# Weight slabs of a decode kernel's last pass, fetched in four half-megabyte pieces through a two-half ring

## The chip, the cores and the metric

The kernel runs on one core of one Trainium2 chip, as one launch. The metric is device time in microseconds (us), as a median of several runs; before the change it is 1956.27 us, the median of three runs (1954.14 to 1961.74). A profile of one further execution shows where that time goes. MB is a million bytes in the rates that the profile states; a "megabyte" of a tile or a slab is 1024 KB.

## The reference

Four layers are applied to one token's vector of 1024 values: attention over a cache, a feed-forward layer, the same attention again, the same feed-forward layer again. All gradients are wanted too, those of the two large caches included.

```python
# attention: 32 query heads, 4 cache groups, 65536 cached rows of 128
q = layernorm(x) @ wq                         # wq: 1024 x 4096
p = softmax(q @ k_cache.T * Dh ** -0.5)
x = x + (p @ v_cache) @ wo                # wo: 4096 x 1024
# feed-forward: w1 1024 x 3584, w2 3584 x 1024
x = x + relu(layernorm(x) @ w1 + b1) ** 2 @ w2 + b2
...
out, vjp = jax.vjp(f, x, k_cache, v_cache, wq, wo, w1, b1, w2, b2)
grads = vjp(grad_out)
```

Each cache is 4 x 65536 x 128 in bf16. Their gradients have the same shape and are summed over both attention layers.

## The kernel before, in words

The work is done in four passes over the two caches with dense stages between them: a forward pass for each attention layer, a backward pass for the second one, and a last pass (`attn_bwd4`, L1268) that does the backward work of the first attention layer and writes the cache gradients of both.

**The last pass.** It walks over 256 items, 64 for each of the four groups, of eight cache columns each. Four items are a block, and one block of either cache is one DMA of 1024 KB into one slot. For each item the V columns are turned on TensorE (`vT`, L1324) and multiplied with the output gradient (`vS`, L1355); the result on VectorE is X (L1373); X and the stored probabilities are turned (L1339), and outer products form the gradients of V and K (`outer16`, L1396), which ScalarE or VectorE (`evac`, L161 and L164) copies from PSUM to slots that GpSimd's queue stores (L1402). At the end `k8` (L1427) multiplies the K columns with X. `pipeline` (L828) emits these stages item by item; a scheduler then sets the order on every engine. So an "item" in what follows is counted by the groups of eight matmuls of L1427 that stand in the built program's order.

**Slots.** All of these tiles lie in one arena of 20 slots of 1024 KB (L255 to L261). `take_one` (L284) gives a load the slot that has been free longest, of those that are not set aside for stores (up to five are). Loads are all issued by SyncE's queue (SP), in order: a load whose slot is still in use holds up those behind it.

**Background work.** `Background.step` (L774) runs once an item. It advances an "urgent" generator by one step; if that step answers "wait", the turn goes on to the "normal" work: outer products of the weight gradients (`g_outer`, L1499, and `g_outer_wide`, L1518, in steps of one `rank2`, L1468). Any other answer uses up the turn. What is left of either is run to its end by `drain` (L808), called from `fill4` (L1837) ten items before the end of the pipeline.

**The urgent work of the last pass** is six products of a vector with a weight block of 2 MB: three of wo (`g_dO`, L953, for the groups still to come) and three of wq (`g_dn`, L980, for the groups that are done). Both go through `g_rowdots` (L565). The weight block comes as two slabs of 1024 KB, each with four rows of 1024 values in every partition, through `slabs` (L433), whose DMA is L450. A row is multiplied with the broadcast vector on VectorE (L586, into `mv_t`, of which there are two buffers), and ScalarE sums the product (L575). In this pass four "wait" steps lie ahead of the first slab's products, after the broadcast's four, and eight between the request of the second slab and its products:

```python
        for kc, slab in slab_it:
            if vbc is None:
                vbc = yield from g_bcast_vec(vcol, nj)
                for _ in range(steps - WAIT_STEPS + 1):
                    yield "wait"
            elif kc % 4 == 0:
                for _ in range(steps):
                    yield "wait"
```

A slab's slot is freed when the generator comes back after its fourth row, and the second slab is then requested into another slot. The functions that the diff touches, and their callers:

Of the kernel before, what the change touches and what calls it, by code (L numbers as in the profile page):

```python
# [10 lines left out]
BF = mybir.dt.bfloat16  # L11
F32 = mybir.dt.float32
ACTF = mybir.ActivationFunctionType
ALU = mybir.AluOpType
AX = mybir.AxisListType
PSUM = bass.MemoryType.PSUM
P = 128
# [3 lines left out]
def kernel(  # L21
# [24 lines left out]
    nc = tc.nc  # L46
# [6 lines left out]
    R = HQ // G  # L53
    F = B_w1.shape[1]
    DC, FC = D // P, F // P
# [10 lines left out]
    TLEAD = 2  # L66
    STORE_STEPS = 5
    WAIT_STEPS = 5
    NSLOT = 12
    NWT = 6  # L70
    NKEEP = [8, 7, 7]
# [3 lines left out]
    vec = ctx.enter_context(tc.tile_pool(name="vec", bufs=1))  # L75
    tmp = ctx.enter_context(tc.tile_pool(name="tmp", bufs=2))
    ktpool = ctx.enter_context(tc.tile_pool(name="ktpool", bufs=4))
    mvs = ctx.enter_context(tc.tile_pool(name="mvs", bufs=2))
# [3 lines left out]
    PS = {}  # L82
# [62 lines left out]
    def add_load(act=0.0, dve=0.0, pe=0.0):  # L145
        load["act"] += act
        load["dve"] += dve
        load["pe"] += pe
# [107 lines left out]
    JW = 2 * J  # L256
    NG = NSLOT + 2 * G
    assert C * R == BLK
# [9 lines left out]
    def plane(lay, g):  # L268

        return NSLOT + G + g if lay else NSLOT + G - 1 - g  # L270

# [155 lines left out]
    def rows_of(W):  # L427
        return W.rearrange("(kc p) n -> p kc n", p=P)
# [4 lines left out]
    def slabs(name, load, nk, kper, ncols, ahead=1, flat=False):  # L433
        pend = deque()
        ks = deque(range(0, nk, kper))

        def fetch():
            k = ks.popleft()
            i = None
            if ks and flat and NOW["wide"] and not odd_one():  # L440
                i = take_pair()
            if i is None:
                kn = min(kper, nk - k)
                sl = Slot(name)
            else:
                kn = min(2 * kper, nk - k)
                ks.popleft()
                sl = Slot(name, at=i, both=True)
            v = sl.t[:, 0:kn * ncols].rearrange("p (k n) -> p k n", n=ncols)
            nc.sync.dma_start(out=v, in_=load(k, kn))  # L450
            pend.append((k, kn, sl, v))

        def gen():
            while ks or pend:
                while ks and len(pend) < ahead:
                    fetch()
                k, kn, sl, v = pend.popleft()
                for kk in range(kn):
                    NOW["slab"] = sl
                    yield k + kk, v[:, kk, :]  # L460
                sl.over = True
                if not sl.users:
                    sl.free()
        g = gen()
        g_fetch = [fetch for _ in range(ahead)]
        return g, g_fetch
# [8 lines left out]
    def wq_slabs(g, ahead=1):  # L475
        v = rows_of(A_wq)
        return slabs("s_wq", lambda k, kn: v[:, k:k + kn, g * 1024:(g + 1) * 1024], DC, 4, 1024, ahead, True)
# [5 lines left out]
    def wo_runs(g):  # L483

        v = A_wo[g * 1024:(g + 1) * 1024, :].rearrange("(p k) n -> p k n", k=8)
        return slabs("s_wo", lambda k, kn: v[:, k:k + kn, :], R, 4, 1024, 1, True)[0]
# [9 lines left out]
    def g_mv(slab_it, nk, nbk, xcol, ps_of, finish, side=None, pre=None, cols=d_cols):  # L496
# [4 lines left out]
        for kc, slab in slab_it:  # L501
            if ps_of is ps_bg and kc % 4 == 0:
                for _ in range(WAIT_STEPS):
                    yield "wait"
# [42 lines left out]
    def g_bcast_vec(vcol, nj):  # L547
        pt = ps_mv([nj, P], F32)
        nc.tensor.transpose(pt[:, :], vcol, ident_f[:, :])
        yield  # L550
        rows = tmp.tile([32, P], BF, name="bc_rows")
        nc.vector.tensor_copy(out=rows[0:nj, :], in_=pt[:, :])
        vbc = mvs.tile([P, nj * P], BF, name="vbc", tag="vbc", bufs=1)
        yield
        for j0 in range(0, nj, 4):
            pg = ps_gg() if PS["pass4"] else ps_tr([P, 512], F32)
            for jj in range(4):
                nc.tensor.matmul(pg[:, jj * P:(jj + 1) * P], lhsT=ident_b[0:nj, j0 + jj:j0 + jj + 1].to_broadcast([nj, P]),
                                 rhs=rows[0:nj, :], start=True, stop=True)
            nc.scalar.copy(out=vbc[:, j0 * P:(j0 + 4) * P], in_=pg[:, 0:512])  # L560
            add_load(act=0.6)
            yield
        return vbc

    def g_rowdots(slab_it, nk, vcol, nj, finish, name):  # L565
        n = nj * P
        y = vec.tile([P, nk], F32, name=name)
        nc.gpsimd.memset(y[:], 0.0)
        vbc = None
        due = None  # L570
        steps = 8 if PS["pass4"] else WAIT_STEPS

        def total(t, kc):
            def f():
                nc.scalar.activation(out=t[:, :], in_=t[:, :], func=ACTF.Copy, accum_out=y[:, kc:kc + 1])  # L575
            return f
        for kc, slab in slab_it:
            if vbc is None:
                vbc = yield from g_bcast_vec(vcol, nj)
                for _ in range(steps - WAIT_STEPS + 1):  # L580
                    yield "wait"
            elif kc % 4 == 0:
                for _ in range(steps):
                    yield "wait"
            t = mvs.tile([P, n], BF, name="mv_t", tag="mv_t", bufs=2)
            nc.vector.tensor_tensor(out=t[:, :], in0=slab, in1=vbc[:, :], op=ALU.mult)  # L586
            add_load(dve=0.1 + n * 0.00054, act=0.42 + n * 0.00083)
            if due is not None:
                due()
            due = total(t, kc)  # L590
            yield
        due()
        yield
        r = finish(y[:, :])
        if r is not None:
            yield from r
        yield
# [299 lines left out]
    def gsl(g):  # L897
        return slice(g * R, (g + 1) * R)
# [35 lines left out]
    def dO_finish(L, g):  # L934
        def fin(y):
            nc.vector.tensor_copy(out=L["dOT"][:, gsl(g)], in_=y)
            prod = tmp.tile([P, R], F32, name="dlt_prod")
            nc.vector.tensor_tensor(out=prod[:], in0=L["dOT"][:, gsl(g)], in1=L["oT"][:, gsl(g)], op=ALU.mult)
            yield
            pd = ps_mv([33, R], F32)  # L940
            nc.tensor.matmul(pd[:, :], lhsT=ones_f[:, 0:33], rhs=prod[:, :], start=True, stop=True)
            yield
            negd = tmp.tile([33, R], F32, name="negd")
            nc.vector.tensor_scalar(out=negd[:], in0=pd[:], scalar1=-1.0, scalar2=None, op0=ALU.mult)
            hi = tmp.tile([33, R], BF, name="negd_hi")
            nc.vector.tensor_copy(out=hi[:], in_=negd[:])
            lo = tmp.tile([33, R], BF, name="negd_lo")
            nc.vector.tensor_tensor(out=lo[:], in0=negd[:], in1=hi[:], op=ALU.subtract)
            nc.vector.tensor_copy(out=L["nd2"][0:1, gsl(g)], in_=hi[0:1, :])
            nc.vector.tensor_copy(out=L["nd2"][32:33, gsl(g)], in_=lo[32:33, :])  # L950
        return fin

    def g_dO(L, dx, g):  # L953
        def fin(y):
            each = tmp.tile([P, R, 8], F32, name="run_own", bufs=1)
            nc.vector.tensor_tensor(out=each[:, :, :], in0=y.unsqueeze(1).to_broadcast([P, R, 8]),
                                    in1=M8[:, :].unsqueeze(2).to_broadcast([P, R, 8]), op=ALU.mult)
            yield
            pt = ps_mv([P, R, 8], F32)
            nc.tensor.matmul(pt[:, :, :].rearrange("p r k -> p (r k)"), lhsT=from_runs[:, :, :].rearrange("p a b -> p (a b)"),  # L960
                             rhs=each[:, :, :].rearrange("p r k -> p (r k)"), start=True, stop=True)
            yield
            own = tmp.tile([P, R, 8], F32, name="run_own", bufs=1)
            nc.vector.tensor_tensor(out=own[:, :, :], in0=pt[:, :, :], in1=eighth[:, :].unsqueeze(1).to_broadcast([P, R, 8]), op=ALU.mult)
            back = tmp.tile([P, R], F32, name="run_o")
            nc.vector.tensor_reduce(out=back[:], in_=own[:, :, :], axis=AX.X, op=ALU.add)
            yield
            yield from dO_finish(L, g)(back[:, :])
        yield from g_rowdots(wo_runs(g), R, dx[:], DC, fin, "%s_dO%d" % (L["name"], g))


    def dn_finish(dn, first):
        def fin(y):
            if first:
                nc.vector.tensor_copy(out=dn[:], in_=y)
            else:
                nc.vector.tensor_tensor(out=dn[:], in0=dn[:], in1=y, op=ALU.add)
        return fin

    def g_dn(L, dn, g, first):  # L980
        yield from g_rowdots(wq_slabs(g)[0], DC, L["dqT"][:, gsl(g)], R, dn_finish(dn, first), "%s_dn%d" % (L["name"], g))


# [894 lines left out]
```

## Time and profile before

| what | value |
|---|---|
| median of three runs | 1956.27 us (1954.14 to 1961.74) |
| the profiled execution: time / span from first to last instruction | 1956.67 us / 1954.7 us |
| TensorE's granted clock, mean of the span | 0.911 |
| busy share: PE / VectorE (DVE) / ScalarE (ACT) / GpSimd | 82% / 60% / 53% / 7% |
| moved by DMA over the whole span | 787.64 MB, mean 403 GB/s |
| last pass, 1195 us to the end at 1955 us | 760 us for 256 items |
| products L586 in the last pass | 48, median 682 ns |
| sums L575 in the last pass | 48, median 1070 ns, and as many reads of the sum, 203 ns |
| SP's waits in the last pass for PE's L1427 / L1324 / for DVE's L586 | 384.4 us (47 times) / 129.3 us (40) / 23.0 us (6) |

The page gives busy time by engine, then the span in 40 slices, then the DMA queues, a chain of what ended last, the costliest groups and the DMA issues. A line of a group names the source line, the engine, the tiles (out<-in), how often, and the mean duration; after the bar stands how long the engine sat idle ahead of these instructions and what ended that. The same can be asked for any stretch of the span, and each engine's instructions can be listed in order of time, with the idle time ahead of each in brackets. A wait there is put down to what came last by the profile; "issue" means that nothing the profile shows ended it.

### The profile page before, as it was taken

How to read it: one execution, taken by the hardware profiler on the slowest of the kernel's cores; microseconds unless marked ns; L12 is line 12 of the kernel's file. 1: busy time of each engine (PE TensorE's matmuls, PEld its weight loads, DVE VectorE, ACT ScalarE, POOL GpSimd, SP SyncE). 2: the span in 40 equal slices, each digit the busy share in tenths (PEclk: the TensorE clock that was granted, in tenths of full speed). 3: DMA queues.
4: the chain of work that ended last, by engine and by line, in shares of the span. 5: the costliest groups of instructions: out<-in, count | busy, mean ns of one | idle time of the engine just before them, and what ended most of it. 6: DMA issues, size and time to landing. Idle time of an engine off the chain costs nothing. (4 is left out here: it accounts for less than half of the span.)

```text
span 1954.7 us, 67155 instructions
## 1 busy us (share of the span) xinstructions
PE 1598.7 (82%) x30319; PEld 1312.0 (67%) x30319; DVE 1167.6 (60%) x2421; ACT 1038.3 (53%) x1600; POOL 141.2 (7%) x321
## 2 busy tenths in 40 slices
PE   6878788687888878887787898888996987687977
PEld 6878778687777778777777785555554554454644
DVE  5655455255455544544454476867776886676866
ACT  3444334254334444435363465766876785576765
POOL 0000000000000000000000001111111211121211
PEclk9989899699899999898998999888888998897997
DMA  9999999999999998899999987999999999899997
GB/s 395 426 426 425 428 428 410 401 399 425 429 425 428 428 412 307 317 427 423 426 426 418 403 321 297 411 404 423 423 424 405 420 423 423 341 423 384 424 422 317
DMA packets 105997, 787.64 MB, mean 403 GB/s; under 512 B 9312, under 2 KB 16494, under 8 KB 42094
## 3 DMA queue, kind: packets, MB, share of 16 engines
q1 hardware_dynamic: 81630, 617.65, 76.6%
q0 software_dynamic: 24080, 165.70, 20.4%
q8 instruction: 237, 3.88, 0.7%
q14 instruction: 50, 0.41, 0.1%
HBM read 617.62 MB, written 165.69 MB: 401 GB/s over the span
## 5 line engine op out<-in xcount | busy, mean ns | idle before, releaser
L164 DVE COPY kt<-ps_tr 128x1024 bf16<-128x1024 bf16 x724 | 496.6, 688 | 439.5 <-PE ps_tr L1012 246.6
L161 ACT CAST arena<-ps_gg 128x1024 bf16<-128x1024 f32 x457 | 444.3, 1011 | 190.9 <-PE ps_gg L1396 147.0
L1012 PE MATMUL ps_tr<-ident_b,arena 128*128 128x128 bf16 x3840 | 309.0, 226 | 39.1 <-DMA arena<-in_A_k_cache_dram 26.6
L161 ACT COPY kt<-ps_tr 128x1024 bf16<-128x1024 bf16 x164 | 171.8, 1053 | 187.1 <-PE ps_tr L1204 118.1
L164 DVE CAST arena<-ps_gg 128x1024 bf16<-128x1024 f32 (+2 forms) x186 | 222.3, 1195 | 79.9 <-PE ps_gg L1396 35.0
L1012 PEld LDWEIGHTS <-arena 128*128 128x128 bf16 x3840 | 232.8, 101 | 47.9 <-DMA arena<-in_A_k_cache_dram 29.4
L1114 PE MATMUL ps_acc<-arena 128*128 128x64 bf16 (+4 forms) x4096 | 205.8, 196 | 61.5 <-DMA arena<-in_A_v_cache_dram 49.3
L1396 PE MATMUL ps_gg<-GG,xt 64*128 64x512 bf16 x1024 | 212.2, 412 | 47.5 <-DVE arena L164 35.0
L1114 PEld LDWEIGHTS <-arena 128*128 128x128 bf16 x4096 | 159.8, 101 | 66.3 <-DMA arena<-in_A_v_cache_dram 53.0
L1324 PE MATMUL ps_tr<-ident_b,arena 128*128 128x128 bf16 x1824 | 177.8, 233 | 30.3 <-DMA arena<-in_A_v_cache_dram 28.4
L1095 ACT ACTIVATE arena<-S_sb,L_negm 128x128 bf16<-128x128 f32 x256 | 165.6, 1003 | 66.0 <-DVE L_negm L1080 65.9
L1030 PE MATMUL ps_sc<-L_qpad,kt 128*128 128x64 bf16 (+7 forms) x3584 | 183.4, 195 | 15.0 <-ACT kt L161 7.1
L1204 PE MATMUL ps_tr<-ident_b,arena 128*128 128x128 bf16 x1920 | 157.1, 228 | 45.0 <-DMA arena<-in_A_v_cache_dram 43.4
L1324 PEld LDWEIGHTS <-arena 128*128 128x128 bf16 x1824 | 117.1, 103 | 86.1 <-issue 52.9
L1030 PEld LDWEIGHTS <-kt 128*128 128x128 bf16 x3584 | 153.3, 100 | 19.4 <-ACT kt L161 9.8
L1204 PEld LDWEIGHTS <-arena 128*128 128x128 bf16 x1920 | 119.2, 102 | 48.9 <-DMA arena<-in_A_v_cache_dram 46.7
L1427 PEld LDWEIGHTS <-arena 128*128 128x128 bf16 x2048 | 93.8, 102 | 62.9 <-issue 41.7
L1095 ACT ACTIVATION_READ_ACCUMULATOR arena<-S_sb,L_negm 128x1 f32 x256 | 128.0, 500 | 0.0
L1396 PEld LDWEIGHTS <-xt 64*128 64x128 bf16 x1024 | 65.1, 94 | 93.6 <-issue 54.7
L575 ACT ACTIVATE mv_t<-mv_t 128x1024 bf16<-128x1024 bf16 x96 | 102.0, 1064 | 41.7 <-DVE mv_t L586 41.6
L1355 PE MATMUL ps_sc<-DOB,kt 128*128 128x64 bf16 (+3 forms) x1824 | 113.6, 199 | 0.0
L1427 PE MATMUL ps_acc<-X,arena 128*128 128x64 bf16 (+3 forms) x1536 | 100.1, 198 | 14.9 <-DMA arena<-in_A_k_cache_dram 14.9
(306 smaller groups left out, 2161.4 us busy)
## 6 DMA issues: line engine op xcount, KB each, us to landing
arena<-in_A_k_cache_dram SPq DMA_DIRECT2D x86, 2048.0 KB, 21.5
arena<-in_A_v_cache_dram SPq DMA_DIRECT2D x83, 2048.0 KB, 21.0
out_dram<-arena POOLq DMA_DIRECT2D x149, 1024.0 KB, 16.5
arena<-in_A_v_cache_dram SPq DMA_DIRECT2D x76, 1024.0 KB, 14.2
arena<-in_A_k_cache_dram SPq DMA_DIRECT2D x76, 1024.0 KB, 15.1
arena<-in_A_wo_dram SPq DMA_DIRECT2D x22, 1024.0 KB, 14.0
arena<-in_B_w_dram SPq DMA_DIRECT2D x21, 1024.0 KB, 7.9
arena<-in_A_wq_dram SPq DMA_DIRECT2D x18, 1024.0 KB, 13.9
```

What stands on the lines that cost most here:

```text
L161: nc.scalar.copy(out=out, in_=in_)
L164: nc.vector.tensor_copy(out=out, in_=in_)
L575: nc.scalar.activation(out=t[:, :], in_=t[:, :], func=ACTF.Copy, accum_out=y[:, kc:kc + 1])
L1012: nc.tensor.transpose(pt[:, i, :], kb8[:, i, :], ident_b[:, :])
L1030: nc.tensor.matmul(state["ps_s"][:, s:s + w, :].rearrange("p a b -> p (a b)"), lhsT=kt[:, i, :], rhs=L["qpad"][:, g, 0:w, :].rearrange("p ...
L1095: nc.scalar.activation(out=E(p, g, c0, SU)[:, :, h], in_=S[:, h, :], func=ACTF.Exp, bias=L["negm"][:, g, su, h:h + 1], scale=SCALE, accum_ ...
L1114: nc.tensor.matmul(ps_o[:, 0:w, :], lhsT=vb8[:, i, :], rhs=E(p, g, c, w), start=(c % SU == 0), stop=(c % SU == SU - 1), skip_group_check=True)
L1204: nc.tensor.transpose(pt[:, i, :], vb8[:, i, :], ident_b[:, :])
L1324: nc.tensor.transpose(pt[:, i, :], vb8[:, i, :], ident_b[:, :])
L1355: nc.tensor.matmul(state["ps_dp"][:, s:s + w, :].rearrange("p a b -> p (a b)"), lhsT=vt[:, i, :], rhs=DOB[:, g, 0:w, :].rearrange("p a b - ...
L1396: nc.tensor.matmul(pg[:, 512 * h:512 * h + 512], lhsT=xt[64 * h:64 * h + 64, j1 // 8 + m, :], rhs=gg[64 * h:64 * h + 64, :, :].rearrange(" ...
L1427: nc.tensor.matmul(ps_dq[:, 0:w, :].rearrange("p a b -> p (a b)"), lhsT=kb8[:, i, :], rhs=X[:, s:s + w, :].rearrange("p a b -> p (a b)"), ...
```

## The change

In the last pass alone, `g_dO` and `g_dn` go to a new generator, `g_rowdots_paced`. It takes one slot and uses its two halves in turn: four pieces of 512 KB (two rows of 1024 values in every partition) are requested at its steps 0, 6, 12 and 18, and a piece's two rows are multiplied 10 and 11 steps after that piece's step of request. The sum of a row follows one step after its product. A step with anything in it uses up the turn, the others answer "wait". The third piece overwrites the first one's half, and the fourth the second's. `g_rowdots` keeps its behaviour in the other passes and loses the branch for this one. The wo view is the same as before, cut in pieces of two rows.

```diff
+    PIECE_EVERY, PIECE_LAND = 6, 10
...
-        steps = 8 if PS["pass4"] else WAIT_STEPS
...
+    def g_rowdots_paced(view, vcol, nj, finish, name):
+        n = nj * P
+        y = vec.tile([P, 8], F32, name=name)
+        nc.gpsimd.memset(y[:], 0.0)
+        sl = Slot("s_piece")
+        buf = sl.t[:, 0:4 * n].rearrange("p (k n) -> p k n", n=n)
+        def fetch(j):
+            k = 2 * j % 4
+            nc.sync.dma_start(out=buf[:, k:k + 2, :], in_=view[:, 2 * j:2 * j + 2, :])
+        def product(kc):
+            t = mvs.tile([P, n], BF, name="mv_t", tag="mv_t", bufs=2)
+            nc.vector.tensor_tensor(out=t[:, :], in0=buf[:, kc % 4, :], in1=vbc[:, :], op=ALU.mult)
+            add_load(dve=0.1 + n * 0.00054)
+            return t
+        def total(kc, t):
+            nc.scalar.activation(out=t[:, :], in_=t[:, :], func=ACTF.Copy, accum_out=y[:, kc:kc + 1])
+            add_load(act=0.42 + n * 0.00083)
+        fetch(0)
+        yield "wait"
+        vbc = yield from g_bcast_vec(vcol, nj)
+        plan, made = {}, {}
+        for j in range(4):
+            if j:
+                plan.setdefault(PIECE_EVERY * j, []).append(lambda j=j: fetch(j))
+            for h in range(2):
+                at = PIECE_EVERY * j + PIECE_LAND + h
+                plan.setdefault(at, []).append(lambda kc=2 * j + h: made.update({kc: product(kc)}))
+                plan.setdefault(at + 1, []).insert(0, lambda kc=2 * j + h: total(kc, made.pop(kc)))
+        for t in range(5, max(plan) + 1):
+            for fn in plan.get(t, ()):
+                fn()
+            yield 0 if t in plan else "wait"
+        sl.free()
+        r = finish(y[:, :])
+        if r is not None:
+            yield from r
+        yield
...
     def g_dO(L, dx, g):
+        if PS["pass4"]:
+            runs = A_wo[g * 1024:(g + 1) * 1024, :].rearrange("(p k) n -> p k n", k=8)
+            yield from g_rowdots_paced(runs, dx[:], DC, fin, "%s_dO%d" % (L["name"], g))
+            return
         yield from g_rowdots(wo_runs(g), R, dx[:], DC, fin, "%s_dO%d" % (L["name"], g))
...
     def g_dn(L, dn, g, first):
+        if PS["pass4"]:
+            yield from g_rowdots_paced(rows_of(A_wq)[:, :, g * 1024:(g + 1) * 1024], L["dqT"][:, gsl(g)], R, dn_finish(dn, first),
+                                       "%s_dn%d" % (L["name"], g))
+            return
         yield from g_rowdots(wq_slabs(g)[0], DC, L["dqT"][:, gsl(g)], R, dn_finish(dn, first), "%s_dn%d" % (L["name"], g))
```

More of the change, by code (lines that the diff above doesn't have):

```diff
@@ L579, in g_rowdots @@
                 vbc = yield from g_bcast_vec(vcol, nj)
-                for _ in range(steps - WAIT_STEPS + 1):
-                    yield "wait"
+                yield "wait"
             elif kc % 4 == 0:
-                for _ in range(steps):
+                for _ in range(WAIT_STEPS):
                     yield "wait"
@@ L593, in g_rowdots @@
         yield
+        r = finish(y[:, :])
[20 more added lines that the diff above has]
+        fetch(0)
+        yield "wait"
+        vbc = yield from g_bcast_vec(vcol, nj)
[12 more added lines that the diff above has]
+        sl.free()
         r = finish(y[:, :])
```

## The prediction

> **What bounds the kernel now.** Nothing ahead of the last pass changes: up to there the built orders of both programs are the same on every engine. So I looked first at the DMA row of the page, 40 slices of the span in tenths, where the last pass begins in the 25th:
>
> ```profile
> DMA  9999999999999998899999987999999999899997
> ```
>
> and then at the last pass alone, by stretches (us; busy us and instructions of each engine, then granted clock, DMA share, GB/s).
>
> ```profile
> 1195.00:1225.00 30.00, 24.76 (x362) 15.54 (x360) 20.40 (x32) 16.55 (x18) 5.70 (x11) 0.89 0.84 320
> 1225.00:1800.00 575.00, 479.67 (x6088) 304.10 (x6085) 413.26 (x736) 400.96 (x480) 99.04 (x191) 0.88 0.99 409
> ...
> 1910.00:1955.00 45.00, 33.79 (x422) 20.53 (x419) 27.45 (x52) 25.19 (x27) 7.56 (x12) 0.77 0.77 305
> ```
>
> From 1225 us on the DMA engines are full (0.99), while no compute engine is; an engine's wait there costs time only if it lets the DMAs run dry. The change moves the same bytes, so its gain is bounded by the DMA idle time that slab loads cause. To find that I listed VectorE in order of time around the slab products and SP around their requests (start, duration, what; in brackets the idle time before).
>
> ```profile
> 1465.51 0.38 SPq L450 DMA_DIRECT2D arena<-in_A_wq_dram  x1
> ...
> 1573.77 0.90 SPq L450 DMA_DIRECT2D arena<-in_A_wo_dram  x1
> ...
> 1666.79 0.38 SPq L450 DMA_DIRECT2D arena<-in_A_wq_dram  x1
> ...
> 1771.35 0.38 SPq L450 DMA_DIRECT2D arena<-in_A_wq_dram  x1
> ```
>
> ```profile
> 1495.99 0.69 DVE L586 TENSOR_TENSOR mv_t<-arena,vbc 128x1024 bf16<-128x1024 bf16 x1 [10.16 <-DMA arena<-in_A_wq_dram]
> ...
> 1588.83 0.69 DVE L586 TENSOR_TENSOR mv_t<-arena,vbc 128x1024 bf16<-128x1024 bf16 x1 [3.89 <-issue]
> ...
> 1686.12 0.69 DVE L586 TENSOR_TENSOR mv_t<-arena,vbc 128x1024 bf16<-128x1024 bf16 x1 [13.96 <-issue]
> ...
> 1790.90 0.69 DVE L586 TENSOR_TENSOR mv_t<-arena,vbc 128x1024 bf16<-128x1024 bf16 x1 [11.55 <-issue]
> ```
>
> Each of the four is the first product of a second slab, 30.5, 15.1, 19.3 and 19.6 us after its request. The profile names the DMA once and "issue" three times; since the other idle times end as long after a request, I take all four for the slab's landing. PE needs VectorE's copies, so it stands too. What the DMAs then do, in steps of 5 us (last two columns):
>
> ```profile
> 1505.00:1510.00 5.00, 4.58 (x70) 3.05 (x68) 4.79 (x8) 4.31 (x6) 1.15 (x2) 0.99 0.77 297
> 1510.00:1515.00 5.00, 3.64 (x42) 2.65 (x42) 3.21 (x6) 3.68 (x6) 0.53 (x1) 0.69 0.96 369
> ...
> 1680.00:1685.00 5.00, 0.00 (x0) 0.00 (x0) 0.00 (x0) 0.00 (x0) 0.00 (x0) 0.50 0.72 301
> 1685.00:1690.00 5.00, 2.00 (x14) 0.95 (x13) 3.65 (x5) 2.96 (x4) 0.53 (x1) 0.50 0.08 30
> 1690.00:1695.00 5.00, 5.00 (x53) 3.08 (x53) 4.12 (x7) 2.09 (x3) 0.00 (x0) 0.50 0.82 280
> ...
> 1790.00:1795.00 5.00, 2.15 (x21) 1.72 (x21) 4.00 (x8) 2.96 (x4) 0.66 (x2) 0.50 0.44 183
> ```
>
> What is missing from a share of 1, times 5 us, is DMA idle time: 1.35 us after the stall of 10.16; 1.4 + 4.6 + 0.9, and 0.15 in the slice after, so 7.05, after that of 13.96; 2.8 after that of 11.55; none after 3.89 (share 1.02). Together **11.2 us**, and a price list for stalls: up to 4 us free, 10 us cost 1.35, 11.6 cost 2.8, 14 cost 7. The DMA queue is worked off during a stall, and only the rest is lost.
>
> **The change part by part.**
>
> 1. *The four stalls go.* First and second pieces stand 12 items or more ahead of their products in the built order; an item takes 760/256 = 2.97 us, so 35.6 us, more than the 30.5 of the slowest slab above. **-11.2 us.**
>
> 2. *Third and fourth pieces bring new ones.* The ten steps are not kept for them. Their request overwrites a half of the ring and waits for the second product on it, while loads run ahead of the compute. In the built order, from the later of that product and the load ahead in SP's queue to the first product on the new piece, I count for the third pieces of the three wq jobs 4, 3 and 3 items, for the fourth 4, 5 and 4; for wo 5.2, 3.8, 4 and 4.6, 4.4, 3.6. So a wq piece has 11.9 or 8.9 us. The landing of one in this stage is not in the trace. From the DMA view of 1200 to 1900 us and, for the size, from the whole page (last column: median us to landing):
>
> ```profile
> arena<-in_A_k_cache_dram SPq DMA_DIRECT2D x58, 1024.0 KB, 15.7
> ...
> arena<-in_A_wq_dram SPq DMA_DIRECT2D x8, 1024.0 KB, 22.9
> ...
> arena<-in_A_wo_dram SPq DMA_DIRECT2D x6, 1024.0 KB, 9.2
> ```
>
> ```profile
> arena<-in_A_k_cache_dram SPq DMA_DIRECT2D x86, 2048.0 KB, 21.5
> ...
> arena<-in_A_k_cache_dram SPq DMA_DIRECT2D x76, 1024.0 KB, 15.1
> ```
>
> Bounds: 22.9 us if the queue ahead sets it and size nothing, 11.5 if it goes with size. K loads gain 6.4 us by halving 2048 KB, so 3.2 for the next halving: I take 22.9 - 3.2 = 19.7, nearest to the wq row. Stalls of the third pieces: 7.8, 10.8, 10.8; by the price list, between its points, 0.8 + 2 x 2.0. The fourth get the third's stall on top of their distance (11.9 + 7.8, 14.9 + 10.8, 11.9 + 10.8) and have landed. A wo piece has 10.7 us at least; even at the 15.1 above it stalls 4.4, free. **+4.9 us**; with 22.9 (stalls 11.0, 14.0, 14.0) 2.2 + 7.1 + 7.1 = 16.4, with 11.5 nothing.
>
> What queues behind: a third piece's request holds the K and V loads behind it in SP's queue, which wait for PE at the same or a later item, so it costs them nothing unless VectorE stands; then they would wait for PE anyway. Twelve more issues at 0.33 to 0.38 us on SP are 4.3 us beside its 384.4 us of waiting for L1427.
>
> The trace's row for many DMAs in flight is the share of 0.99 at 409 GB/s; by it, cutting 12 slabs in 24 pieces costs nothing. A rule of the Trainium skill speaks against the change: "DMA: Bandwidth & Descriptors", section "Measured", asks for DMAs of at least 1 MiB, and its section on the anatomy of one DMA gives each a fixed 2.0 us. If the 12 added ones paid that one after the other, the sum would be 24 us longer; by the row I put it at 0.
>
> 3. *Outer products move to the end.* A paced job answers "wait" less often: it uses up 13 steps of its plan, 4 of the broadcast and 1 at the end, 18 where the old one used 14, so with 3 x 5 steps of finishing both 123 where it was 99. The normal work has 150 steps, and from item 1 of its pacing to `fill4` are some 257: 257 - 123 = 134 is too few, 257 - 99 = 158 was enough. `drain` runs the rest at once. The built order shows it: after the last L1427 stand 40 matmuls of L1474 and 4 stores of L1514, against 16 and none. Those 24 matmuls are 12 copies at 1.01 (ACT) or 1.2 us (DVE), 6.6 us on two engines, and some ten small copies (L161 and L164 for rowa, 0.57 to 0.68) another 3: 9 us in a stretch of 45 us where DMA is at 0.77 and the copies set the pace. In return 4 MB leave the full stage, at 424 GB/s 9.4 us or so. **-0.4 us**; bounds -5 (the copies hide beside other work) and +9 (the full stage's end is set by K loads and gives nothing back).
>
> 4. *Order of the first 64 items.* Two K loads stand at no distance by items (32 and 52), where before the least was 1.8. The only row of that kind is 1290 to 1295 us, share 0.77. I add one more such, **+1.2 us**; bounds 0 and 4.
>
> 5. *Work.* 48 products and 48 sums as before; one slot held 24 to 28 items against two for as many in all. 0.
>
> Sum against the profiled execution: 1956.67 - 11.2 + 4.9 - 0.4 + 1.2 = **1951.2 us** (0.3% less). Its time is 0.4 above the median, so nothing is rescaled.
>
> **The rivals.**
>
> A. *All of it pays.* Half pieces land in 11.5 us, no stall over 4 us is left, and the moved copies find room: 1956.67 - 11.2 - 4.5 = 1941. For it: the wo slabs' 9.2 us. Against: wq slabs took 19 us and more each time that VectorE stood.
>
> B. *The ring's waits replace the slabs' waits and cost more (slower).* Place: third pieces of the three wq jobs. If a half lands in 25 us, as between the slabs' 22.9 and the 30.5 of one, the stalls are 13.1, 16.1, 16.1, by the price list 5.5 + 10.8 + 10.8 = 27.1 instead of 4.9: 1973.4. It decides from a landing of about 21.5 us, where the three cost what the four slabs did. For it: those distances of 3 and 4 items. Against: half the size.
>
> C. *The tail takes back the gain.* Part 3 at its worse end: 1951.2 + 9.4 = 1960.6. For it: DMA share 0.77 there, so bytes don't set its length. Against: bytes set the stage ahead.
>
> D. *It doesn't do what it says.* True in part for third and fourth pieces, and counted above.
>
> **How the numbers follow.** 0.5% (9.8 us) is about what a measurement of this kernel can tell from no change; its bounds are 1946.9 and 1966.5. Forecast 0.43, of which 0.16 falls below 1946.9; A 0.22; B 0.20; C 0.15. Faster 0.16 + 0.22 = 0.38, same 0.27 + 0.15 = 0.42, slower 0.20. The range reaches from a little under A to B: 1939 to 1973. The forecast's own range is 1943 to 1960.
>
> **What would show it.** Part 1: no idle time over 4 us ahead of a first or second piece's product, and no 5 us slice at 0.08. Part 2: idle time ahead of the first product on third wq pieces, 8 to 11 us, and requests of them landing in about 20. Part 3: stores of L1514's kind after the last dqT, and a longer stretch from there to the end (17.8 us before, from 1936.9). Wrong if third pieces stand for over 13 us, if DMA is below 0.95 in the stage for another reason, or if the tail grows by more than the stage shrinks.

## The result, and the profile after

The changed kernel takes **1985.33 us** (median of five runs, 1982.15 to 1988.07) against 1956.84 for the kernel before in the same comparison: ratio 1.0152, 95% interval 1.0135 to 1.0169, so 28.5 us slower. That is past the upper end of the range on record (1973) and past rivals B and C. The profiled execution took 1986.77 us, its span is 1984.7.

First the DMA row of the changed kernel's page, in slices of about 50 us, then the two large DMA queues of both pages (packets, MB, share of 16 engines' span):

```profile
DMA  9999999999999997899999988999999999998985
```

```profile
q1 hardware_dynamic: 82590, 617.65, 75.6%
q0 software_dynamic: 24080, 165.70, 20.1%
```

```profile
q1 hardware_dynamic: 81630, 617.65, 76.6%
q0 software_dynamic: 24080, 165.70, 20.4%
```

The bytes are equal, the second fence is that of before. With the two small queues (0.7% and 0.0 or 0.1%) the DMAs are idle for 3.6% of 1984.7 us, 71 us, where before it is 2.2% of 1954.7, 43 us (a tenth of a per cent, to which the page rounds each queue, is 2 us; stretches at full load read 1.01 or 1.02, so these sums serve to compare, and the true idle time is somewhat longer). So 28 of the 30 us by which the span grew are **DMA idle time**, and not slower transfers. Where it lies, by the stretches of the last pass (busy us and instructions of each engine, granted clock, DMA share, GB/s):

```profile
1225.00:1800.00 575.00, 471.18 (x6140) 303.36 (x6137) 409.19 (x736) 395.12 (x467) 103.92 (x194) 0.89 0.99 409
...
1910.00:1955.00 45.00, 37.08 (x467) 23.25 (x468) 29.04 (x67) 26.30 (x30) 4.50 (x7) 0.77 0.68 269
1955.00:1985.00 30.00, 14.15 (x69) 4.10 (x68) 14.25 (x22) 12.54 (x16) 5.93 (x9) 0.50 0.51 211
```

The full stage has the same 0.99 and 409 GB/s as before, to the digit, although all four stalls of part 1 are gone. The loss is behind it: 1910 to 1955 us at 0.68 for 0.77 is 4 us, and 30 us are new, at half share: 14.7. From 1800 to 1910 (0.99 for 1.01) come 2 more. Some 5 lie ahead of the last pass, where both programs are the same: its first V turn (L1374, L1324 before) starts at 1219.4 us for 1214.2, and in the traces of all the runs below between 1212.7 and 1223.7. That part belongs to the executions, not to the change.

The weight products still stall. VectorE's idle time ahead of L613, the product (L586 before), in the last pass (us, times), and two of the stalls with their requests on SP:

```profile
  DMA arena<-in_A_wo_dram: 27.7, 5
  DMA arena<-in_A_wq_dram: 24.6, 4
```

```profile
1533.56 0.69 DVE L613 TENSOR_TENSOR mv_t<-arena,vbc 128x1024 bf16<-128x1024 bf16 x1 [7.36 <-DMA arena<-in_A_wq_dram]
...
1725.72 0.69 DVE L613 TENSOR_TENSOR mv_t<-arena,vbc 128x1024 bf16<-128x1024 bf16 x1 [8.11 <-DMA arena<-in_A_wq_dram]
```

```profile
1512.82 0.38 SPq L609 DMA_DIRECT2D arena<-in_A_wq_dram  x1
...
1709.72 0.46 SPq L609 DMA_DIRECT2D arena<-in_A_wq_dram  x1
```

All nine are third or fourth pieces, 52.3 us in all and none over 9.2, where four stalls made 39.6 before. The third wq piece of 1709.72 us was multiplied 16.0 us after its request. The DMA issues of 1200 to 1900 us (last column: median us to landing):

```profile
arena<-in_A_wo_dram SPq DMA_DIRECT2D x12, 512.0 KB, 14.5
arena<-in_A_wq_dram SPq DMA_DIRECT2D x12, 512.0 KB, 16.7
```

And the end. The last dqT (L1232, L1182 before) stands at 1944.53 us, so 40.2 us are left to the end of the span; before it was 1936.90, and 17.8:

```profile
1944.53 0.17 DVE L1232 SCALAR_TENSOR_TENSOR L_dqT<-dqa,L_rZ 128x8 f32<-128x8 f32 x1
```

```profile
1936.90 0.17 DVE L1182 SCALAR_TENSOR_TENSOR L_dqT<-dqa,L_rZ 128x8 f32<-128x8 f32 x1
```

The groups of these last stretches, first of the changed kernel, then of the one before (after the bar busy us, mean ns, then the engine's idle time ahead of them by releaser):

```profile
L165 DVE CAST arena<-ps_gg 128x1024 bf16<-128x1024 f32 x13 | 15.9, 1225 | 9.2 <-PE ps_gg L1524 6.4 <-PE ps_gg L1446 2.6
L162 ACT CAST arena<-ps_gg 128x1024 bf16<-128x1024 f32 x13 | 13.1, 1012 | 10.1 <-PE ps_gg L1524 8.8 <-PE ps_gg L1446 1.4
L1524 PE MATMUL ps_gg<-rowb,rowa 2*128 2x512 bf16 x40 | 12.3, 584 | 5.6 <-DVE arena L165 1.8 <-ACT rowa L162 1.3 <-ACT rowb L162 1.1
```

```profile
L161 ACT CAST arena<-ps_gg 128x1024 bf16<-128x1024 f32 x7 | 7.1, 1012 | 4.4 <-PE ps_gg L1474 3.4 <-PE ps_gg L1396 1.0
L164 DVE CAST arena<-ps_gg 128x1024 bf16<-128x1024 f32 x4 | 4.9, 1222 | 0.6 <-PE ps_gg L1474 0.5
L1474 PE MATMUL ps_gg<-rowb,rowa 2*128 2x512 bf16 x16 | 3.9, 426 | 2.1 <-ACT arena L161 1.8 <-DVE arena L164 0.3
```

26 copies of 1024 values against 11. The two copying engines stand idle for 9.2 and 10.1 us beside 15.9 and 13.1 us of copies, mostly for PE; PE waits for their copies. It is a chain that alternates, at the half clock, as a stretch of the chain that ended last shows (start, duration, engine, what it writes):

```profile
1957.19 0.62 PE ps_gg L1524
...
1957.84 1.02 ACT arena L162
...
1958.90 0.63 PE ps_gg L1524 x2
...
1959.55 1.02 ACT arena L162
```

**Theory T**, from these lines: some 22 of the 28 us are outer products left to that end, because the paced jobs use up 24 turns more. **Rival R**: the ring's waits (nine stalls) are the cause, and the end only shows what is late. A third part, that nobody had named, came out on the way: where the products stand.

### The profile page after: what moved, and what is told of

The parts are those of the page before. It is cut to its first block, busy times and chain, and to the rows that moved or that the text cites. A ratio compares the mean times of both kernels' runs of the same rounds, so it can differ in the third digit from the quotient of the medians.

```text
span 1984.7 us, 67209 instructions
## 1 busy us (share of the span) xinstructions
PE 1601.3 (81%) x30319; PEld 1315.7 (66%) x30319; DVE 1169.8 (59%) x2419; ACT 1038.3 (52%) x1602; POOL 144.6 (7%) x321
## 3 DMA queue, kind: packets, MB, share of 16 engines
q0 software_dynamic: 24080, 165.70, 20.1%
## 5 line engine op out<-in xcount | busy, mean ns | idle before, releaser
L162 ACT CAST arena<-ps_gg 128x1024 bf16<-128x1024 f32 (+1 forms) x454 | 440.0, 1009 | 220.8 <-PE ps_gg L1446 167.7
L162 ACT COPY kt<-ps_tr 128x1024 bf16<-128x1024 bf16 x168 | 175.9, 1053 | 189.4 <-PE ps_tr L1254 118.0
L165 DVE CAST arena<-ps_gg 128x1024 bf16<-128x1024 f32 (+2 forms) x189 | 226.9, 1203 | 77.9 <-PE ps_gg L1446 40.5
L1374 PE MATMUL ps_tr<-ident_b,arena 128*128 128x128 bf16 x1824 | 175.5, 231 | 33.4 <-DMA arena<-in_A_v_cache_dram 25.1
L1374 PEld LDWEIGHTS <-arena 128*128 128x128 bf16 x1824 | 116.5, 103 | 82.5 <-issue 52.9
L1080 PEld LDWEIGHTS <-kt 128*128 128x128 bf16 x3584 | 152.9, 100 | 19.3 <-ACT kt L162 10.2
L1477 PE MATMUL ps_acc<-X,arena 128*128 128x64 bf16 (+3 forms) x1536 | 93.9, 197 | 25.5 <-DMA arena<-in_A_k_cache_dram 25.5
L1405 PEld LDWEIGHTS <-kt 128*128 128x128 bf16 x1824 | 84.4, 102 | 40.8 <-issue 39.8
## 6 DMA issues: line engine op xcount, KB each, us to landing
out_dram<-arena POOLq DMA_DIRECT2D x149, 1024.0 KB, 13.4
arena<-in_A_wo_dram SPq DMA_DIRECT2D x16, 1024.0 KB, 17.8
```

The source lines that it names most:

```text
L162: nc.scalar.copy(out=out, in_=in_)
L165: nc.vector.tensor_copy(out=out, in_=in_)
L1080: nc.tensor.matmul(state["ps_s"][:, s:s + w, :].rearrange("p a b -> p (a b)"), lhsT=kt[:, i, :], rhs=L["qpad"][:, g, 0:w, :].rearrange("p ...
L1374: nc.tensor.transpose(pt[:, i, :], vb8[:, i, :], ident_b[:, :])
L1405: nc.tensor.matmul(state["ps_dp"][:, s:s + w, :].rearrange("p a b -> p (a b)"), lhsT=vt[:, i, :], rhs=DOB[:, g, 0:w, :].rearrange("p a b - ...
L1477: nc.tensor.matmul(ps_dq[:, 0:w, :].rearrange("p a b -> p (a b)"), lhsT=kb8[:, i, :], rhs=X[:, s:s + w, :].rearrange("p a b -> p (a b)"), ...
```

## The experiments

Medians and ratios to the kernel before, run beside each (its medians were 1956.2 to 1958.0). "Left" counts the outer-product matmuls that stand behind the last `k8` in the built order; "stalls" is VectorE's idle time that a weight load (or "issue") ended ahead of the products; "DMA idle" is taken from the queues' shares of the one profiled execution (in e13 and e14 that one took 1963 and 1961 us, less than the median, in e5 and e8 1967 and 1978, more). The stalls are of that one execution too: e15 and e18, which leave the slabs as they were, show 24 us for the 39.6 of before.

| run | median us | ratio (95%) | left | stalls us | DMA idle us |
|---|---|---|---|---|---|
| before | 1956.8 | 1 | 16 | 39.6 | 43 |
| after | 1985.3 | 1.0152 (1.0135 to 1.0169) | 40 | 52.3 | 71 |
| e1 steps spared | 1973.0 | 1.0072 (1.0055 to 1.0090) | 16 | 68.5 | 49 |
| e2 before, turns used up | 1977.1 | 1.0098 (1.0080 to 1.0116) | 40 | 29.5 | 63 |
| e3 two slots | 1984.0 | 1.0135 (1.0117 to 1.0153) | 40 | 0 | 67 |
| e4 two slots, steps spared | 1961.2 | 1.0019 (1.0006 to 1.0033) | 16 | 0 | 49 |
| e5 before, longer lead | 1961.1 | 1.0023 (1.0007 to 1.0038) | 16 | 17.6 | 49 |
| e6 whole slabs, spared | 1960.8 | 1.0015 (1.0001 to 1.0030) | 16 | 2.8 | 43 |
| e7 before, 12 turns | 1971.1 | 1.0066 (1.0050 to 1.0081) | 24 | 20.1 | 59 |
| e8 ring, 93 turns | 1969.2 | 1.0060 (1.0045 to 1.0076) | 16 | 73.9 | 59 |
| e9 before, shorter lead | 1962.6 | 1.0031 (1.0017 to 1.0044) | 16 | 30.4 | 51 |
| e10 before, steps spared | 1967.9 | 1.0059 (1.0040 to 1.0078) | 16 | 7.5 | 49 |
| e11 ring 8/8, spared | 1972.3 | 1.0076 (1.0058 to 1.0094) | 16 | 50.4 | 57 |
| e12 whole slabs, 123 turns | 1991.3 | 1.0173 (1.0153 to 1.0193) | 40 | 4.4 | 74 |
| e13 two slots, 93 turns | 1969.1 | 1.0064 (1.0044 to 1.0083) | 16 | 0 | 45 |
| e14 whole slabs, 93 turns | 1967.4 | 1.0058 (1.0040 to 1.0076) | 16 | 10.6 | 49 |
| e15 before, pace 242 | 1953.7 | 0.9992 (0.9976 to 1.0008) | 16 | 24.3 | 43 |
| e16 plan, four in a row | 1954.9 | 0.9987 (0.9976 to 0.9998) | 16 | 17.3 | 43 |
| e17 before, spread | 1971.1 | 1.0070 (1.0053 to 1.0088) | 16 | 56.7 | 55 |
| e18 before, pace 232 | 1954.7 | 0.9982 (0.9973 to 0.9992) | 16 | 24.4 | 43 |

### The turns and the ring apart: e1 to e4

e1, the changed kernel with no turn used up by a plan's step:

```diff
-            yield 0 if t in plan else "wait"
+            yield "wait"
```

> The changed kernel, but a paced job answers wait on every step of its plan, so that the scheduler's turn goes on to the outer products also on the 13 steps that issue something. The ring and its ten steps stay. In the built order 16 matmuls of the outer products stand behind the last k8, as in the kernel before, against 40 in the changed one. Theory T (the tail: leftover outer products, 40.2 us from the last dqT to the end against 17.8): the tail falls back to about 18 us, so 1985.3 - 22.4 = 1963 us. Rival R (the ring: stalls on pieces cost the time, and the tail is only where it shows): the ring is as it was, so within 5 us of 1985.

Measured 1973.0, between the two: 12 us gained, not 22. The end fell to 18.8 us as T has it; the stage ahead of it became longer. DMA idle time explains only 6 of its 17 us above before: the DMAs were also busy for 97.5% of 1972.1 us, 11 us longer than before, for the same bytes.

e2, the kernel before with 24 more turns used up:

```diff
-                for _ in range(steps):
-                    yield "wait"
+                for k in range(steps):
+                    yield 0 if PS["pass4"] and k < 4 else "wait"
```

> The kernel before, with its two slabs of 1024 KB, but four of the eight waits between the second slab's request and its products use up the turn: 6 x 4 = 24 turns, as many as the change takes. The distance of the slab stays. In the built order 40 outer-product matmuls stand behind the last k8, as in the changed kernel. Theory T: the tail grows from 17.8 to about 40 us, so 1956.8 + 22.4 = 1979 us. Rival R: no ring, no piece, so 1957, within 5 us.

Measured 1977.1: **+20 us from the turns alone**, with no piece and no ring. Its last dqT and the groups behind it are those of the changed kernel, almost to the number, 40.5 us to the end:

```profile
1932.96 0.17 DVE L1182 SCALAR_TENSOR_TENSOR L_dqT<-dqa,L_rZ 128x8 f32<-128x8 f32 x1
```

```profile
L164 DVE CAST arena<-ps_gg 128x1024 bf16<-128x1024 f32 x13 | 15.9, 1223 | 9.7 <-PE ps_gg L1474 7.1 <-PE ps_gg L1396 2.6
L161 ACT CAST arena<-ps_gg 128x1024 bf16<-128x1024 f32 x13 | 13.1, 1012 | 10.4 <-PE ps_gg L1474 9.0 <-PE ps_gg L1396 1.4
```

The dqT came 3.9 us earlier than before, so the stage did give something back, but 4 us for 22.7 at the end.

e3, the changed kernel with a second slot, so that no request waits for a product:

```diff
+            if j % 2 == 0:
+                sls.append(Slot("s_piece"))
+                buf[j // 2] = sls[-1].t[:, 0:4 * n].rearrange("p (k n) -> p k n", n=n)
...
+            if kc % 4 == 3:
+                sls[kc // 4].free()
```

> The changed kernel, but the third and fourth pieces go into a second slot instead of over the first and second: no request waits for a product on the ring. Steps and turns as in the change. Theory T: the tail stays at 40 us; at most the 7 us by which the stage ahead of it grew go, so 1978 to 1986. Rival R: the nine stalls of 52.3 us on weight pieces go with the ring, so 1957 to 1960.

Measured 1984.0: **no weight stall is left, and 1.3 us are gained**, less than the two intervals can tell apart. R is out. What the engines do in place of stalling on weights is seen at 1639 us, PE first, then the DMAs:

```profile
1639.62 0.72 PE L1377 MATMUL ps_tr<-ident_b,arena 128*128 128x128 bf16 x5 [4.53 <-DMA arena<-in_A_v_cache_dram]
```

```profile
1640.00:1645.00 5.00, 5.00 (x43) 2.79 (x41) 2.66 (x4) 2.02 (x2) 0.53 (x1) 0.50 0.33 138
1645.00:1650.00 5.00, 4.85 (x80) 3.11 (x79) 4.35 (x7) 3.05 (x4) 0.53 (x1) 0.89 0.51 215
```

PE waits for a V load, and the DMAs then run dry just as after a weight stall (5.8 us in these two slices). Here the DMAs set the pace, and the engines wait for some load; without the weight it was the next one.

e4 has both edits (the diffs of e1 and e3).

> Both edits: a second slot for the third and fourth pieces, and wait on every step. Theory T: the tail at 18 us, and stalls gone, so 1950 to 1958. Rival R: also about 1957; this run sizes what the ring costs once the tail is right, as the difference to the first run: 7 us if the growth of the stage is the ring's, 0 to 2 us if stalls of less than 10 us are free.

Measured 1961.2, above T's 1950 to 1958. e1 and e4 differ in the ring alone, and by 12 us: with these spared turns the ring does cost something, against 1.3 us with the change's turns (e3) and none with 93 (e8 and e13 below). Why its price depends on the turns was not found.

### The predicted steps one at a time: e5 to e8

e5, the slab stalls of before shortened by asking earlier, and nothing else:

```diff
-        steps = 8 if PS["pass4"] else WAIT_STEPS
+        steps = 14 if PS["pass4"] else WAIT_STEPS
...
-                for _ in range(steps - WAIT_STEPS + 1):
+                for _ in range(4 if PS["pass4"] else 1):
```

> The kernel before, with 14 waits instead of eight between the request of a second slab and its products; waits do not use up turns, so the outer products stay where they were (16 matmuls behind the last k8). This does the first step of the prediction alone. Step 1 as predicted (four stalls cost 11.2 us of DMA idle time): 1956.8 - 11.2 = 1946. Theory T, in the form that the last runs gave it (a stall on a weight slab costs nothing, since with it gone the engines wait for a K or V load instead): 1957, within 4 us.

Measured 1961.1: no gain, rather 4 us lost. The stalls that are left (6.0, 10.4 and 1.3 us) cost 2 us by the price list, so by it 9 should have been gained. **They aren't there**, unless holding the second slab six items longer costs about as much; e16 below, which holds it only one or two items longer than before, speaks against that.

e6, e4's plan with whole slabs:

```diff
-            if j % 2 == 0:
-                sls.append(Slot("s_piece"))
...
+            if j % 2:
+                return
+            sls.append(Slot("s_piece"))
...
-            nc.sync.dma_start(out=buf[j // 2][:, k:k + 2, :], in_=view[:, 2 * j:2 * j + 2, :])
+            nc.sync.dma_start(out=buf[j // 2], in_=view[:, 2 * j:2 * j + 4, :])
```

> As the run with two slots and spared steps, but the weights come as two slabs of 1024 KB, requested at the plan's steps 0 and 12, ten steps ahead of their first product; products and sums stay on their steps. It differs from that run (1961.2) in the size of the DMAs alone. If the 512 KB pieces themselves cost DMA time (4.1 us more busy time than before by that run's packets): 1957. If size is nothing: 1961.

Measured 1960.8, as e4: the size of the DMAs costs nothing here. The Trainium skill's rule that the prediction weighed ("DMA: Bandwidth & Descriptors", "Measured") speaks against pieces below 1 MiB; that table is for DMAs issued from GpSimd, where the weight loads here come from SP, and no run here shows that price.

e7, e2's diff with `k < 2`: half its turns.

> The kernel before, with two waits of each job made to use up the turn: 99 + 12 = 111 turns, against 123 of the change and 107 that there are to spare. It is a smaller dose of the run with used-up steps (+20). In the built order 24 outer-product matmuls stand behind the last k8 (16 before, 40 changed), and 46 from the 240th k8 on (32 and 62). Theory T: in proportion, 8/24 to 14/30 of 20 us, so 1964 to 1966. If a turn costs as such, wherever there are spare ones: half, 1967; if only the turns' place in the tail counts by a threshold: 1957.

Measured 1971.1, +13, above all three figures: more than the share of matmuls left behind (8 of the 24 more) gives, with 31.9 us from the last dqT to the end. What is left fits a threshold at the 107 turns to spare (16 matmuls at up to 99 turns, 24 at 111, 40 at 123); the first 12 turns cost 13 us, the next 12 some 7.

e8, the changed kernel with the turn used up on product steps alone:

```diff
-            yield 0 if t in plan else "wait"
+            yield 0 if t >= PIECE_LAND and (t - PIECE_LAND) % PIECE_EVERY < 2 else "wait"
```

> The changed kernel, its ring and steps included, but only the eight product steps of a job use up the turn, not the five that issue a request or a sum: 123 - 30 = 93 turns, fewer than the 107 to spare. 16 outer-product matmuls stand behind the last k8. Theory T: tail of 18 us; the ring as in the run with all steps spared, so 1973 if the 12 us between that run and the one with two slots are the ring's, 1961 if they came from two pieces of work in one item. Rival R (ring alone): 1985.

Measured 1969.2, between T's two figures: 16 us of the 28.5 are back with the ring as it was, five turns a job fewer. 12 us above before stay open.

### What is left over: e9 to e12

e9, e5's diff with 4 for 14.

> The kernel before, with four waits instead of eight ahead of a second slab's products: each of the six second slabs is wanted four items (some 12 us) earlier against its request, the turns as before. By step 1's price list (14 us of stall cost 7) stalls that are up to 12 us longer would cost far more than the 11.2 us of before: over 1980. Theory T (engines wait for the DMAs in any case, and a weight stall takes the place of other waits): the stalls grow, the time stays at 1957 to 1962, until a stall outlasts what is queued.

Measured 1962.6. The over 1980 rested on longer stalls, as did T's expectation, and the stalls did not grow: they went from 39.6 to 30.4 us (5.8, 11.3 and 13.4). By the price list these cost 9 us, 2 less than before; measured are 6 more. So the run says little of long stalls, but the list fails on it too.

e10, the kernel before with `yield "wait" if PS["pass4"] else None` after each product.

> The kernel before, but the eight product steps of a job answer wait: the turn goes on to the outer products. Slabs, requests and distances as before; 16 outer-product matmuls behind the last k8 (as before) and 20 from the 240th on (32 before). The variants with two slots, planned slabs and spared steps took 1961: if their 4 us above the kernel before come from outer products moved forward, this one takes 1961 too; if from slots held longer, 1957.

Measured 1967.9, above both figures: giving the turns away is no gain by itself, and the old slabs take it worse than the plan does. Why was not found.

e11, e1 with `PIECE_EVERY, PIECE_LAND = 8, 8`.

> As the first run (ring, all steps spared, 1973), but a piece every eight steps, multiplied eight steps after its request instead of every six and ten: the third piece's request stands five to seven items behind the products that free its half, instead of one. If the 12 us between the first run and the one with two slots (1961) are the ring's wait, most of them go: 1961 to 1965. If they come from anything else in that kernel: 1973.

Measured 1972.3. Inconclusive: the edit did not take the ring's wait away. SP's piece requests wait for a product (L613) for 32.1 us, 9 times, against 25.1 us, 9 times, in e1, and the pieces still stall for 50.4 us.

e12, e6 with the change's own line for the turns (`yield 0 if t in plan else "wait"`).

> As the run with planned whole slabs (1960.8), but the steps of the plan use up the turn as in the change: the plan, the turns and the leftover (40 matmuls behind the last k8) are the change's, while slabs and slots are the old ones. Theory T, with the two runs before it (20 for the turns): 1960.8 + 20 = 1981. If the 512 KB pieces are what sets the two-slot run (1984) above the run with used-up turns alone (1977): 1977.

Measured 1991.3: the turns cost 30 us here, 10 more than T had. Without ring and without pieces this is slower than the change.

### At equal turns: e13 to e18

e13 is e8 with e3's second slot, e14 is e6 with e8's line for the turns, and e15 the kernel before with `bg.steps = len(ITEMS[3]) - 14` for `- 4`.

> As the run with the ring in which only the product steps use up the turn (1969.2), but with a second slot for the third and fourth pieces: the ring is the one difference, the turns are 93 as there (99 in the kernel before), the tail has no leftover. If the ring's stalls cost what is left beyond the turns: 1957 to 1961. If the rest is the sensitivity of the stage to any shift of the order: 1965 to 1973, or anything between.

> As the run beside it with two slots, but two whole slabs of 1024 KB at steps 0 and 12: the kernel before with the change's plan, and nearly its turns. If only the turns and the ring cost anything: 1957 to 1961, and equal to the run beside it. If the plan itself (a request ten steps ahead, sums one step later) costs: above the run beside it or equal to it, and both above 1961.

> The kernel before with the outer products paced over ten items less (242 for 252): the same work, turns, slabs and distances, each step of the outer products a little earlier, no leftover. A placebo: 1957 (within 3 us) if the stage does not mind such shifts, so that 4 to 11 us in the other runs have causes of their own; 1961 to 1968 if moving the outer products by a few items costs as much by itself.

Measured 1969.1, 1967.4 and 1953.7. With the same 93 turns, ring (e8, 1969.2), two slots and whole slabs are equal, so at these turns neither the ring nor the pieces cost anything; the shifted pace is no cost. The plan itself stays 11 us above before.

e16 is e14 with a slab's four products in a row:

```diff
-                at = PIECE_EVERY * j + PIECE_LAND + h
+                at = 12 * (j // 2) + PIECE_LAND + 2 * (j % 2) + h
...
-            yield 0 if t >= PIECE_LAND and (t - PIECE_LAND) % PIECE_EVERY < 2 else "wait"
+            yield 0 if t >= PIECE_LAND and (t - PIECE_LAND) % 12 < 4 else "wait"
```

> As the run with planned whole slabs and product steps that use up the turn (1967.4), but the four products of a slab stand on four steps in a row, as in the kernel before, instead of two and two, six steps apart; requests at steps 0 and 12. If the spreading of the products over the items makes the 11 us: 1957 to 1961. If the plan's early request, with two slots held at once, makes them: 1967.

e17 is the reverse, the kernel before with its products two and two:

```diff
             due = total(t, kc)
             yield
+            if PS["pass4"] and kc % 4 == 1:
+                for _ in range(4):
+                    yield "wait"
```

> The kernel before, with four waits between the second and the third product of each slab: products two and two, six steps apart, as in the change's plan; slabs, requests and turns as before. If the spreading makes the 11 us: 1965 to 1970. If not: 1957 to 1961.

Measured **1954.9 and 1971.1**: taking the spreading out of the plan gains 12.5 us, putting it into the kernel before costs 14.4. Neither edit moves the products alone: a slab is freed four steps earlier in e16 and four later in e17, and e17 also makes a job eight steps longer and lets the sum of each slab's second product wait for the third. The spreading too is paid as DMA idle time; the queues of e17:

```profile
q1 hardware_dynamic: 81630, 617.65, 76.3%
q0 software_dynamic: 24080, 165.70, 20.2%
```

With 0.7% and 0.0% of the small queues, 2.8% of a span of 1965.9 us: 55 us, 12 more than before, while no more is left to the end (18.9 us from the last dqT).

e18 is e15 with `- 24`.

> The kernel before, with the outer products paced over twenty items less (232 for 252), after the run with ten less at 1953.7 (ratio 0.9992, interval 0.9976 to 1.0008). If earlier outer products take something out of the end of the pass: 1948 to 1953. If that run was no gain: 1954 to 1960.

Measured 1954.7, ratio 0.9982 (0.9973 to 0.9992). e16 and e18 are thus 0.1 to 0.2% faster than the kernel before, e16 barely clear of no change: two versions that beat both kernels, the one before by 2 to 4 us of its 1957 in the ratio.

## Why the prediction was wrong

The change taken apart, one property from line to line:

| kernel | median us | step |
|---|---|---|
| before | 1956.8 | |
| e16: requests by plan, four products in a row, 93 turns | 1954.9 | -1.9 |
| e14: products two and two | 1967.4 | +12.5 |
| e12: 13 steps use up the turn for 8 (123 turns) | 1991.3 | +23.9 |
| e3: 512 KB pieces in two slots | 1984.0 | -7.3 |
| after: the ring | 1985.3 | +1.3 |

In another order (e14, e13, e8, after) the pieces cost 1.7 us, the ring 0.2 and the turns 16.1, so the turns' price lies between 16 and 24. In that order the 34 us between the forecast of 1951.2 and the measured time are: step 1 short by 9, step 3 by 16 to 17, step 5 by 12.5 and the pieces by 2, less some 6 that steps 2 and 4 put too high.

**Step 1 (the four stalls go, -11.2) failed.** The stalls on first and second pieces did go, as it said; the time did not follow. e5 shortens the stalls and gains nothing, e9's are shorter too and it loses 6 us, e16 has two left (9.4 and 7.9 us), worth 2 by the list, and gains 1.9 where the list has 9, e3 has no stall at all and nearly the changed kernel's time; e13 has none either, and e8's time. The price list read DMA idle time that stood behind a stall as the stall's own. What the runs show in its place is that it belongs to the full stage: a V or K load takes the stall's place (e3 at 1639 us), and DMA idle time stays at 43 to 49 us in every kernel of up to some 1961 us.

**Step 2 (+4.9)** had the mechanism right: third wq pieces stall for 4.0, 8.1 and 5.1 us where 7.8, 10.8 and 10.8 were worked out. That this is half to three quarters of it, and not less, is in part luck: they landed after 13.1, 16.0 and 10.4 us for 19.7, and had less time than counted, so two errors offset in part. wo pieces stall longer than said, one fourth wq piece too. The price is +1.3 (after against e3), within the noise, and 0 at 93 turns (e8 against e13), if 12 with spared turns (e1 against e4). Rival B falls for the change as built.

**Step 3 (outer products move to the end, -0.4) is the term that was mis-sized most**, and rival C, which named it, was too small at 1960.6. Its count was right (150 steps, 134 turns). It put the end at +9 us, from 12 copies shared by two engines and some small ones, and let the full stage give 9.4 back. Measured: the end grows by 22.4 us (17.8 to 40.2), and by 22.7 in e2, where the stage gives 3.9 back. In place of copies that keep two engines busy stands the chain shown above, in which a copy waits for its matmuls and they wait for an earlier copy: 15 copies more (12 of the weights, 3 of leftover outer products of the caches), which at 22.4 us is 1.5 us each on average, the small copies between them included. Nor did the stage give anything back in the changed kernel: the last dqT stands 7.6 us later than before, 5 of them from the pass's later start. So the prediction's own sign of being wrong, a tail that grows by more than the stage shrinks, was met.

One part of that is the clock. The row of 1955 to 1985 us has it at 0.50, and a matmul of the outer products took 584 ns there for 426 before; 40 times 158 ns is 6.3 us at most for these matmuls. The Trainium skill ("TensorE: Matmul & The Clock Gate", "Part 1: The HAM clock gate") has the clock at half until TensorE was busy for some 3.4 us on end. The row agrees: PE is busy for 14.15 of 30 us, between waits. In the slices of e3 above it took longer: PE is busy for all of 1640 to 1645 us, and the clock stands at 0.50 throughout.

**Step 4 (first 64 items, +1.2)**: no price seen. From 1225 to 1300 us the changed kernel's DMA share is 1.01, before 0.99.

**Step 5 (work, 0)** is where a whole term is missing. The number of products and sums is the same, but they stand two and two over 30 steps instead of four and four over 24, and that costs 12.5 to 14.4 us (e16 against e14, e17 against before). The prediction gave the plan's spacing no price. Why the spread products cost so much is **not settled**: they cost DMA idle time in the stage, but which wait makes it was not traced to its end. PE's waits for K and V loads (1200 to 1930 us) sum to 80.2 us in e14 and 64.6 in e16; in e17 and before they are 50.9 and 47.9, and the weight stalls differ instead (56.7 and 39.6). Slots held for longer are one candidate (e5 holds one of two slabs for six items longer and loses 4 us); e9, which holds them for less and loses 6, speaks against it. Nor do the terms add up freely: 20 for the turns in the old kernel, 24 to 30 in the plan with whole slabs, 12 to 16 with the ring; the -7.3 of the pieces is there at 123 turns and not at 93 (e13, e14).

## What to carry to other kernels

In this stage, where the DMAs are full, a stall ahead of one instruction wasn't worth the DMA idle time behind it: move that one wait and see whether the time follows, before a change is built on it. Price a plan's spacing too: the same products on other steps cost more here than the ring. Where background work shares turns with other jobs, count the turns against the work; what does not fit lands at the end, and is to be priced there as a chain (matmul, copy, matmul at a half clock), not as busy time shared by engines. And in a kernel with equal bytes, compare the DMA queues' shares first: their idle time followed the span in most runs here (not in e1).

## What the runs showed that was not expected

Pieces of 512 KB land only little sooner than loads twice their size in the full stage: 14.5 and 16.7 us, beside 15.6 for K blocks and 14.4 for V blocks of 1024 KB in the same stretch; the wo pieces took longer than the whole wo slabs of before (9.2). And a shorter lead did not lengthen the stalls (e9: 30.4 us with four items, 39.6 with eight, 17.6 with 14, one execution each): a request's place in the program does not fix when SP issues it, since SP waits for slots ahead of it.
